# Tile 2 of queries and keys transposed by DMA, and five more products in TensorE's start-up

## The chip, the cores and the metric

The kernel runs on one core of one Trainium2 chip. The metric is the time of one execution on the device, in microseconds (us); lower is better. Every kernel is executed several times, and the median is compared.

## The reference

Two layers are chained. The first is attention with 8 batches, 8 heads, 576 positions and 64 values a head, in which a query sees only the keys at most 32 positions away. The second is a feed-forward layer over all 8 x 576 = 4608 tokens of 512 values, with a gated activation between its two products.

```python
scores = scale * np.matmul(q, k.transpose(0, 1, 3, 2))
mask = np.abs(pos[:, None] - pos[None, :]) <= 32
scores = np.where(mask, scores, -1000000000.0)
attn = softmax(scores)
x = np.matmul(attn, v)                   # (8, 8, 576, 64) -> (4608, 512)
h = x @ w_in                             # 512 -> 2048
out = (h * (1.0 / (1.0 + np.exp(-1.702 * h)))) @ w_out   # 2048 -> 512
```

## The kernel before

**Units, tiles, windows.** The 4608 tokens are laid end to end and shifted by 32. A *unit* is 128 tokens (36 units), a *window* two units, a *tile* of queries and keys 512 tokens or four units. For one unit the work is: `scores(u)` (TensorE, 32 small products of keys by queries into two PSUM banks, then exp on ScalarE), `band(u)` (VectorE multiplies by the 0/1 mask), `values(u)` (TensorE, weights times values), `norm(u)` (VectorE divides), `x_T(u)` (the result is transposed, by TensorE or by a DMA), `layer1` (TensorE, then the activation on ScalarE) and `layer2` or, from unit 8 on, `product`/`keep`/`result` (a scheme with seven products in place of eight). The first four units are masked in another way: `blind(u)` multiplies an identity by a tile `neg` of 0 and -30000 into the two score banks, and the scores are added on top of that.

**Queries and keys.** Scores need queries and keys with the head's values on the partitions, so both are transposed into two rings `qT` and `kT` of 1536 tokens (three tiles). Scores of unit u read the keys of unit u and 64 more, and queries from 32 to 160 after the unit's start. There are two ways to fill the rings.
- *By TensorE*: `load_heads` (four neighbouring tokens a partition, pieces of four tokens), `pair_heads` (a copy that puts two heads side by side), and `rows_T` (four transposes on TensorE into a PSUM bank, then one copy into the ring: VectorE for keys, ScalarE for queries). Tiles "A" and "B" (together tile 0), 1 and 2 go this way.
- *By transfer*: `load_rows` (one token a partition, chunks of 128 tokens) and `rows_X` (a DMA transpose of one chunk from SBUF into the ring, issued on SP). Tiles 3 to 8 go this way.

All loads are cast from f32 on their way and are issued on POOL's queue. SP issues the DMA transposes and the output stores; it is in order, so that a transpose whose load has not landed holds whatever stands behind it.

**The order of the work** is written out by hand: there is no scheduler, and each engine's instructions run in the order of the program text. `head()` holds the loads, units 0 to 6, layer 1 of windows 0 to 2 and layer 2 of units 0 to 3. `window(w)` follows from w = 4 on; window 4 begins with the scores of units 7, 8 and 9, all of which read tile 2. `feed(w)` issues transposes for later windows; in window 4 it also copies the first 64 keys and 32 queries of tile 3 to the ring's end (L714, L715), which the scores of unit 11 read. Near the start, `keep_busy` issues products of zeros, whose results nobody reads.

**PSUM.** Eight banks under four tags: "h" (2), "o" (1), "a" (4), "t" (1). Tile B's eight groups of transposes take turns on "h", "t" and "o", and wait for the copies out of them.

Of the kernel before, what the change touches and what calls it, by code (L numbers as in the profile page):

```python
# [21 lines left out]
SQ = 64  # L22
# [5 lines left out]
class _Kernel:  # L28
# [181 lines left out]
    def setup_neg(self):  # L210

        pool = self.nc.gpsimd
        self.neg = self.cst.tile([128, 2, SQ], BF16, name="neg")
        pool.memset(self.neg, 0.0)
        for b in range(2):
            for half in range(2):
                sign = 1 if half == b else -1
                ap = self.neg[64 * half:64 * half + 64, b, :]
                pool.affine_select(out=ap, in_=ap, compare_op=ALU.is_ge, fill=-30000.0, base=0,  # L219
                                   pattern=[[-sign, SQ]], channel_multiplier=sign)  # L220

    def blind(self, u):

        sc = self.sc[u] = [self.bank("a", [128, 8, SQ], F32, f"sc{eo}") for eo in range(2)]
        neg = self.neg.rearrange("k (o b) s -> k o b s", o=1).to_broadcast([128, 4, 2, SQ])
        for eo in range(2):
            self.nc.tensor.matmul(sc[eo].rearrange("k (h b) s -> k h b s", b=2), self.ident, neg,
                                  start=True, stop=False, skip_group_check=True)
# [192 lines left out]
    def head(self):  # L421

        nc, dve, act, pool = self.nc, self.nc.vector, self.nc.scalar, self.nc.gpsimd
        for hp in range(2):
            self.load_raw("k", hp, nc.sync)
            self.load_raw("q", hp, act)
        self.setup()
        for c in "kq":
            self.load_heads("A", c, (4, 8))
        self.setup_neg()  # L430
        for m in range(3):
            self.load_v(m)
        for c in "kq":
            self.load_heads("B", c)
        self.load_v(3)
        self.load_v(4, 0)
        for c in range(4):
            self.load_w_in(c)
        self.odd_v(2, pool)
        self.odd_v(3, pool)  # L440
        for c in (0, 2):
            self.load_w_out(c)
        self.setup_mask()
        self.cut_mask()
        for c in "kq":
            self.load_heads(1, c)
        self.load_w_out(1)
        self.load_v(4, 1)
        for m in range(5, 7):
            self.load_v(m)  # L450
        self.load_w_out(3)
        self.load_v(7)
        for c in "kq":
            self.load_heads(2, c)
        self.keep_busy(8)
        for hp in range(2):
            self.pair_heads("k", "A", hp, dve, self.stage["k", "raw", hp])
            self.pair_heads("q", "A", hp, act, self.stage["q", "raw", hp])
        for hp in range(4):
            self.rows_T("k", "A", hp, "ht"[hp % 2], dve)  # L460
            self.rows_T("q", "A", hp, "ho"[hp % 2], act)
            if hp < 2:
                self.blind(hp)
        self.scores(0)
        self.scores(1)
        self.odd_v(0, dve)
        self.odd_v(1, act)
        self.keep_busy(3, "h")
        self.values(0, "hh")
        self.norm(0)  # L470
        self.keep_busy(3, "o")
        self.x_T(0, "t", act)
        self.keep_busy(1, "o")
        self.values(1, "oa")
        self.norm(1)
        self.keep_busy(4, "a")
        self.x_T(1, "a", act)
        self.blind(2)
        self.blind(3)
        self.keep_busy(1, "h")  # L480
        for hp in range(4):
            self.pair_heads("k", "B", hp, dve)
        for hp in range(2):
            self.pair_heads("q", "B", hp, dve)
        for hp in range(4):
            self.rows_T("k", "B", hp, "htho"[hp], dve)
            if hp < 2:
                self.pair_heads("q", "B", hp + 2, dve)
            self.rows_T("q", "B", hp, "hoth"[hp], act)
        self.scores(2)  # L490
        self.scores(3)
        self.layer1(0, 0)
        self.values(2)
        self.norm(2)
        self.layer1(0, 1)
        self.values(3)
        self.norm(3)
        self.x_T(2, "t")
        self.layer1(0, 2, "a")
        self.x_T(3, "o")  # L500
        self.layer1(0, 3)
        for d in range(4):
            self.layer1(1, d)
        dve.tensor_copy(self.v_first, self.ve[0][0:64])
        dve.tensor_copy(self.k_first, self.kT[:, :, 0:64])
        dve.tensor_copy(self.q_first, self.qT[:, :, 0:32])
        for n in range(4):
            self.w_sums(n, 0)
        for c in "kq":
            for hp in range(4):  # L510
                self.pair_heads(c, 1, hp, dve)
        for t, d in ((0, 4), (0, 5), (1, 4), (1, 5), (0, 6), (0, 7), (1, 6), (1, 7)):
            self.layer1(t, d)
        l2 = [(lambda c=c, u=u: self.layer2(u, c, "hhot"[u], (dve, act)[u % 2])) for c in range(4) for u in range(4)]

        def run(n):
            for _ in range(n):
                l2.pop(0)()

        run(4)  # L520
        for hp in range(4):
            self.rows_T("k", 1, hp, "a", dve)
            self.rows_T("q", 1, hp, "a", act)
            run(1)
        self.scores(4)
        self.scores(5)
        for m in range(4, 7):
            self.odd_v(m, dve)
        self.band(4)
        run(3)  # L530
        self.band(5)
        run(1)
        self.values(4)
        self.norm(4)
        self.scores(6)
        run(1)
        self.gelu_table()
        self.values(5)
        self.norm(5)
        self.band(6)  # L540
        run(1)
        self.x_T(4, "a", act)
        run(1)
        self.x_T(5, "a", act)
        run(1)
        for c in "kq":
            for hp in range(4):
                self.pair_heads(c, 2, hp, pool)
        self.load_v(8)
        self.load_v(9)  # L550
        self.load_v(10)
        for c in "kq":
            self.load_rows(c, 3, (0, 1))
        self.layer1(2, 0)
        self.values(6)
        self.norm(6)
        for n in range(2):
            self.w_sums(n, 1)
        for d in range(1, 3):
            self.layer1(2, d)  # L560
        self.x_T(6, "a")
        self.layer1(2, 3)
        for hp in range(4):
            self.rows_T("k", 2, hp, "t", dve)
            if hp in (1, 2):
                self.w_sums(hp + 1, 1)
            self.rows_T("q", 2, hp, "o", act)
            self.layer1(2, 4 + hp)
        for m in (7, 8, 9):
            self.odd_v(m, dve)  # L570
        for m in (11, 12, 13):
            self.load_v(m)
        for c in "kq":
            self.load_rows(c, 3, (2, 3))
        for c in "kq":
            self.rows_X(c, 3, (0, 1))

    def window(self, w):
        nc, dve, sp = self.nc, self.nc.vector, self.nc.sync
# [193 lines left out]
```

## Time and profile before

| | us |
|---|---|
| median of 8 runs | 293.97 |
| lowest, highest | 293.18, 295.66 |
| profiled execution, its own time | 293.88 |
| its span, first to last instruction | 292.2 |
| TensorE busy | 285.6 (98%) |
| share of TensorE in the chain of waits | 92% |

The span is what the profile's times count from; the rest of the execution's own time lies around it. The page cuts the span in 40 slices of 7.3 us and gives each engine's busy share in tenths. The chain of waits is followed back from the last instruction: at every step to what released it. PE is TensorE's products, PEld its weight loads, DVE is VectorE, ACT ScalarE, SP the engine that only issues transfers. A transfer's time to landing counts from its issue to the semaphore that tells of its end. The chain, the timelines and the transfers are shown where the prediction uses them.

### The profile page before, as it was taken

How to read it: one execution, taken by the hardware profiler on the slowest of the kernel's cores; microseconds unless marked ns; L12 is line 12 of the kernel's file. 1: busy time of each engine (PE TensorE's matmuls, PEld its weight loads, DVE VectorE, ACT ScalarE, POOL GpSimd, SP SyncE). 2: the span in 40 equal slices, each digit the busy share in tenths (PEclk: the TensorE clock that was granted, in tenths of full speed). 3: DMA queues.
4: the chain of work that ended last, by engine and by line, in shares of the span. 5: the costliest groups of instructions: out<-in, count | busy, mean ns of one | idle time of the engine just before them, and what ended most of it. 6: DMA issues, size and time to landing. Idle time of an engine off the chain costs nothing.

```text
span 292.2 us, 9542 instructions
## 1 busy us (share of the span) xinstructions
PE 285.6 (98%) x4020; PEld 234.8 (80%) x4020; DVE 188.8 (65%) x552; ACT 185.2 (63%) x306; POOL 104.4 (36%) x146
## 2 busy tenths in 40 slices
PE   7989999999999999999999999999999999999995
PEld 2568765875888888888888888888888888888884
DVE  3653467787586858585858585858585858583353
ACT  4667547685776767676767675757575757575330
POOL 8875533998536351633333434242000000000000
PEclk9999999999999999999999999999999999999999
DMA  9999999999999999999999999999925230303012
GB/s 147 143 205 206 199 185 161 172 124 137 175 143 179 152 154 156 145 152 166 151 164 152 151 136 152 143 167 122 179 36 147 37 105 8 104 10 103 2 72 72
DMA packets 145291, 38.83 MB, mean 133 GB/s; under 512 B 129888, under 2 KB 140896, under 8 KB 145248
## 3 DMA queue, kind: packets, MB, share of 16 engines
q0 software_dynamic: 97696, 18.16, 87.5%
q1 hardware_dynamic: 47104, 19.67, 39.9%
q8 instruction: 31, 0.51, 0.7%
q10 hardware_dynamic: 448, 0.39, 0.5%
q14 instruction: 12, 0.10, 0.1%
HBM read 36.96 MB, written 9.44 MB: 159 GB/s over the span
## 4 chain that ended last, share of the span: by engine, by line
PE 92%; DMA 3%; POOL 2%; DVE 1%; issue 0%; ACT 0%; POOLq 0%; DVEq 0%
PE h_ps L313 43%; PE o_ps L375 32%; PE o_ps L325 7%; PE sc L245 4%; PE pv L273 4%; DMA qs<-in_q_dram 3%; PE tp L179 1%; POOL ve L160 1%; PE tp L300 1%; POOL ks L137 0%; DVE qc L105 0%; DVE o_sb L393 0%; POOL neg L219 0%; ACT qT L105 0%; DVE kT L105 0%
## 5 line engine op out<-in xcount | busy, mean ns | idle before, releaser
L313 PE MATMUL h_ps<-xT,w_in_sb 128*128 128x256 bf16 x1152 | 135.1, 273 | 0.0
L315 ACT ACTIVATE g<-h_ps 128x512 f16<-128x512 f32 x144 | 85.5, 595 | 73.7 <-PE h_ps L313 72.4
L313 PEld LDWEIGHTS <-w_in_sb 128*128 128x128 bf16 x1152 | 112.2, 98 | 13.4 <-DMA w_in_sb<-in_moe_w_in_dram 0.2
L160 POOL DMA_DIRECT2D ve<-in_v_dram x40 | 34.0, 857 | 76.6 <-PE pv L273 53.0
L375 PEld LDWEIGHTS <-gs 128*128 128x128 f16 x480 | 45.8, 98 | 6.0 <-issue 0.3
L375 PE MATMUL o_ps<-w_sum,gs 128*128 128x256 f16 x360 | 44.5, 273 | 0.0
L251 ACT ACTIVATE p<-sc 128x512 bf16<-128x512 f32 x72 | 37.2, 603 | 2.7 <-PE sc L245 2.5
L375 PEld LDWEIGHTS <-g 128*128 128x128 f16 x360 | 34.1, 98 | 4.5 <-ACT g L315 0.2
L352 DVE TENSOR_TENSOR gs<-g 128x512 f16<-128x512 f16 x30 | 12.7, 425 | 37.7 <-ACT g L315 37.6
L285 DVE TENSOR_TENSOR x<-pv,rec 128x256 bf16<-128x256 f32 x72 | 30.6, 424 | 2.5
L375 PE MATMUL o_ps<-w_out_sb,g 128*128 128x256 f16 x240 | 29.0, 273 | 0.0
L105 DVE COPY part<-o_ps 128x256 f32<-128x256 f32 x45 | 19.1, 424 | 13.0 <-PE o_ps L375 11.6
L393 DVE TENSOR_TENSOR o_sb<-o_ps,part 128x256 f32<-128x256 f32 x45 | 19.0, 422 | 12.0 <-PE o_ps L375 11.4
L262 DVE TENSOR_TENSOR p<-p,mask 128x512 bf16<-128x512 bf16 x64 | 25.0, 431 | 0.6 <-ACT p L251 0.6
L147 POOL DMA_DIRECT2D qs<-in_q_dram x27 | 23.0, 871 | 4.8 <-DMA ks<-in_k_dram 3.4
L147 POOL DMA_DIRECT2D ks<-in_k_dram x27 | 22.7, 854 | 4.4 <-DMA ve<-in_v_dram 4.0
L325 PE MATMUL o_ps<-w_out_sb,g 128*128 128x512 f16 x96 | 23.2, 380 | 0.0
L105 DVE COPY vo<-ve 64x528 bf16<-64x528 bf16 x65 | 20.7, 318 | 3.5 <-DMA ve<-in_v_dram 2.0
L251 ACT ACT_TABLE_LOAD x15 | 19.2, 1283 | 0.3
L412 ACT ACT_TABLE_LOAD x15 | 19.2, 1283 | 0.3
L284 DVE RECIPROCAL rec<-pv 128x4 f32<-128x4 f32 x72 | 12.6, 175 | 9.7 <-PE pv L273 9.7
L273 PEld LDWEIGHTS <-p 128*64 128x64 bf16 x576 | 11.3, 110 | 6.1 <-DVE p L262 3.6
(70 smaller groups left out, 246.3 us busy)
## 6 DMA issues: line engine op xcount, KB each, us to landing
out_dram<-o_sb SPq DMA_DIRECT2D x34, 256.0 KB, 3.0
ve<-in_v_dram POOLq DMA_DIRECT2D x32, 128.0 KB, 6.6
ks<-in_k_dram POOLq DMA_DIRECT2D x22, 128.0 KB, 7.4
qs<-in_q_dram POOLq DMA_DIRECT2D x22, 128.0 KB, 12.2
w_in_sb<-in_moe_w_in_dram POOLq DMA_DIRECT2D x4, 512.0 KB, 11.4
w_out_sb<-in_moe_w_out_dram POOLq DMA_DIRECT2D x4, 512.0 KB, 12.8
ve<-in_v_dram POOLq DMA_DIRECT2D x8, 64.0 KB, 6.9
ks<-in_k_dram POOLq DMA_DIRECT2D x7, 64.0 KB, 9.5
```

The lines of the kernel that those rows point to most:

```text
L105: (eng.copy if eng is self.nc.scalar else eng.tensor_copy)(out, in_)
L147: self.nc.gpsimd.dma_start(self.stage[key][off:off + m, n], src[b, :, s:s + m, :].rearrange("h s d -> s h d"))
L160: self.nc.gpsimd.dma_start(self.ve[m % NV][off:off + n, :, :self.D], self.v[b, :, s:s + n, :].rearrange("h s d -> s h d"))
L251: nc.scalar.activation(p[:, eo], sc[eo], AF.Exp, scale=self.scale)
L262: self.nc.vector.tensor_mul(pv, pv, msk.to_broadcast([128, 4, 2, SQ]))
L273: nc.tensor.matmul(acc[half][blk * 64:blk * 64 + 64, hh, :], p[:, h % 2, h // 2 * 2 + blk, :], vt[:, h, :D + 1], start=(hh == 0), stop=(hh ...
L285: nc.vector.tensor_mul(x[:, hs, :], acc[half][:, :, :D], rec[:, hs, :].to_broadcast([128, 4, D]))
L313: nc.tensor.matmul(hps[:, i, :], self.w_in_sb[:, kr, ff * 128:(ff + 1) * 128], self.xT[t][:, kr, :], start=(i == 0 and kr == 0), stop=(i = ...
L315: nc.scalar.activation(self.g[t][:, ffs[0]:ffs[1] + 1:ffs[1] - ffs[0], :], hps, AF.Gelu_apprx_sigmoid)
L325: nc.tensor.matmul(o_ps, self.g[t][:, ff, s * 128:(s + 1) * 128], self.w_out_sb[:, ff, :], start=(ff == 0), stop=(ff == self.NFF - 1))
L375: nc.tensor.matmul(self.part[t, key], x, y, start=(first and k == 0), stop=(k == 7), skip_group_check=True)
L412: self.nc.scalar.activation(self.spark, self.spark, AF.Gelu_apprx_sigmoid)
```

## The change

Three things are changed, all in `head()`.

1. Tile 2 is loaded with `load_rows` (8 transfers, chunks 0 and 1 of keys and queries, then 2 and 3) in place of `load_heads` (4 transfers), and `rows_X` transposes it by 8 DMA transposes on SP, which stand in the program behind the copies `v_first`, `k_first` and `q_first`. Its eight `pair_heads` copies on POOL and its eight `rows_T` on TensorE, VectorE and ScalarE are gone.
2. Loads move in POOL's queue: v of units 8 to 11 behind tile 2's loads; v of units 12 and 13 and then the whole of tile 3 to where the pairing copies of tile 2 stood. The DMA transposes of tile 3's first half move ahead of the last four `layer1` of window 2, and the last two `w_sums` on VectorE follow them.
3. A new `refill(u, n)` repeats `blind`'s mask product n times into the banks of unit u. As `start=True` overwrites the bank with the same values, the scores are the same. Four such products on unit 3 stand around the third key pair of tile B (one ahead, three behind), and a `keep_busy` ahead of tile B's transposes issues two products in place of one.

```diff
+    def refill(self, u, n):
+        neg = self.neg.rearrange("k (o b) s -> k o b s", o=1).to_broadcast([128, 4, 2, SQ])
+        for i in range(n):
+            self.nc.tensor.matmul(self.sc[u][i % 2].rearrange("k (h b) s -> k h b s", b=2), self.ident, neg,
+                                  start=True, stop=False, skip_group_check=True)
...
-        for c in "kq":
-            self.load_heads(2, c)
+        for chunks in ((0, 1), (2, 3)):
+            for c in "kq":
+                self.load_rows(c, 2, chunks)
...
-        self.keep_busy(1, "h")
+        self.keep_busy(2, "h")
...
         for hp in range(4):
+            if hp == 2:
+                self.refill(3, 1)
             self.rows_T("k", "B", hp, "htho"[hp], dve)
+            if hp == 2:
+                self.refill(3, 3)
...
+        for m in range(8, 12):
+            self.load_v(m)
+        for chunks in ((0, 1), (2, 3)):
+            for c in "kq":
+                self.rows_X(c, 2, chunks)
         for n in range(4):
             self.w_sums(n, 0)
...
-        for c in "kq":
-            for hp in range(4):
-                self.pair_heads(c, 2, hp, pool)
-        self.load_v(8)
-        self.load_v(9)
-        self.load_v(10)
-        for c in "kq":
-            self.load_rows(c, 3, (0, 1))
+        for m in (12, 13):
+            self.load_v(m)
+        for chunks in ((0, 1), (2, 3)):
+            for c in "kq":
+                self.load_rows(c, 3, chunks)
...
         self.layer1(2, 3)
-        for hp in range(4):
-            self.rows_T("k", 2, hp, "t", dve)
-            if hp in (1, 2):
-                self.w_sums(hp + 1, 1)
-            self.rows_T("q", 2, hp, "o", act)
-            self.layer1(2, 4 + hp)
+        for c in "kq":
+            self.rows_X(c, 3, (0, 1))
+        for n in range(2, 4):
+            self.w_sums(n, 1)
+        for d in range(4, 8):
+            self.layer1(2, d)
         for m in (7, 8, 9):
             self.odd_v(m, dve)
-        for m in (11, 12, 13):
-            self.load_v(m)
-        for c in "kq":
-            self.load_rows(c, 3, (2, 3))
-        for c in "kq":
-            self.rows_X(c, 3, (0, 1))
```

## The prediction

> **What bounds the kernel now.** First the page: busy shares, then the slices.
>
> ```profile
> PE 285.6 (98%) x4020; PEld 234.8 (80%) x4020; DVE 188.8 (65%) x552; ACT 185.2 (63%) x306; POOL 104.4 (36%) x146
> ...
> PE   7989999999999999999999999999999999999995
> ```
>
> A busy PE alone proves little, so I read the chain of waits next. Of its 292.2 us, 92% are TensorE (PE), and from 18 us to 287 us every piece is a PE piece. So what matters is the work in PE's queue, and each product taken out there is worth its chain time. Around the edit the chain reads (start, length, what):
>
> ```profile
> 56.85 0.45 PE tp L179 x8
> 57.30 0.87 PE h_ps L313 x8
> 58.17 0.45 PE tp L179 x8
> 58.62 0.87 PE h_ps L313 x8
> 59.49 0.45 PE tp L179 x8
> 59.94 0.87 PE h_ps L313 x8
> 60.81 0.45 PE tp L179 x8
> 61.26 0.87 PE h_ps L313 x8
> 62.13 0.73 PE sc L245 x64
> 62.86 2.69 PE o_ps L325 x12
> 65.56 0.38 PE sc L245 x32
> ```
>
> The four `tp` pieces are tile 2's transposes; `sc` at 62.13 are the scores of units 7 and 8, at 65.56 those of unit 9. They read tile 2. The timeline of PE shows the second place of the change, the only hole of note after 6 us (the last bracket is idle time and what ended it):
>
> ```profile
> 15.24 0.38 PE L418 MATMUL junk<-idle 128*128 128x512 bf16 x1
> 15.55 0.29 PE L179 MATMUL tp<-ident,kc 64*128 64x64 bf16 x4
> ...
> 16.07 0.28 PE L179 MATMUL tp<-ident,qc 64*128 64x64 bf16 x4
> 16.36 0.27 PE L179 MATMUL tp<-ident,kc 64*128 64x64 bf16 x4
> 17.23 0.27 PE L179 MATMUL tp<-ident,qc 64*128 64x64 bf16 x4 [0.59 <-DVE kT L105]
> ```
>
> Last the transfers, because tile 2 will depend on them. SP issues the DMA transposes one by one; tile 3's first four:
>
> ```profile
> 61.62 2.73 SPq L154 DMA_TRANSPOSE kT<-ks  x2
> 64.44 3.49 SPq L154 DMA_TRANSPOSE qT<-qs  x2
> ...
> DMA to landing us min/median/max: 6.5/7.9/9.3
> ...
> DMA to landing us min/median/max: 2.4/2.4/4.0
> ```
>
> The first landing line is that of all transposes into kT up to 110 us, the second of xT's from 215 to 270 us, when no load runs any more. A transpose takes 2.4 us when alone and 6.5 to 9.3 beside the loads.
>
> **What the Trainium skill says.** "DMA: Bandwidth & Descriptors", section "Issuing engines are not separate DMA queues": transfers issued by SP and by POOL end on the same 16 DMA engines and interleave. The trace agrees (2.4 against 7.9 us above). The same page, "Specifications", asks for at least 512 B per piece for full rate; tile 2's pieces shrink from 512 B to 128 B in SBUF. The trace agrees: from 57.5 to 62.5 us it moved 5642 such packets, 0.71 MB, 0.14 MB/us, against 0.49 MB in 2.5 us, 0.20 MB/us, in the 512 B pieces from 45 us. "TensorE: Matmul & The Clock Gate", Part 1: the clock halves after about one idle window (some 3.4 us, free-running), and Part 4 says that transposes do not count as busy in the same way. The trace shows the half rate only at the start (eight products of 512 columns in 3.27 us); at 12.84 us four take 1.04 us. It shows no fall of the clock near 16 us. The refills can protect against one in other executions, but this trace does not show it.
>
> **Part 1: tile 2's transposes leave TensorE.** 4 head pairs x (k and q) x 4 = 32 products of 219 ns, pipelined to 4 x 0.45 = **1.80 us** of the chain. Nothing else replaces them in PE's queue: a gain of 1.80 us, if tile 2 is in time. Gone too are 4 copies of 0.69 us on VectorE, 4 of 0.58 us on ScalarE, and on POOL 2.28 + 2.67 us of pairing copies. All of these lay beside PE and are worth nothing directly. The gelus behind layer 1's products (0.60 us each against 0.87 us of PE) keep up; the exp of unit 7 shifts with PE.
>
> **Part 2: five more products of 512 columns.** Mask products at 14.19 us were spaced 0.26 us apart. One refill fits ahead of the third k pair (free since 16.19) and makes it 0.1 us late, which is covered, since its copy waits for VectorE until 17.45. Three refills last 0.78 us, from about 16.57 to 17.35; the q pair behind them could start at 17.23. The extra junk product moves the first transposes from 15.55 to some 15.67, with VectorE busy to 15.97 anyway. Cost: 0 (all in holes) to 0.3 us (every overhang passed on to scores 2); I take **0.1**. A gain is not excluded: the runs spread from 293.18 to 295.66, and if a clock dip were behind the upper ones, the median could fall by up to 0.8 us, to its fastest run. I take 0 and keep 0.8 for the low end.
>
> **Part 3: the transfers.** On POOL, tile 2's loads become 8 issues of some 0.88 us (7.0 us) in place of 4 (0.59 + 0.88 + 0.58 + 0.77 = 2.8 us). POOL sat idle for 7.00 us before the first pairing copy, so the issues hide. It never seems to have more than eight transfers under way (the issue at 29.32 follows the landing, at 29.0, of the one eight back). v 8 to 11 move ahead, v 12, 13 wait for values 4 and 5 (49.5 us), with tile 3's loads queued behind them. Before, v 8 was issued only at 53.49.
>
> When is tile 2 there? The load ahead of it, v 7, lands at 35.13 + 10.6 = 45.8. A load of 128 tokens is 1024 pieces; at 5642 in 5 us that is 0.91 us alone; beside transposes I saw six such loads land from 66.3 to 75.4, 1.5 us each. So: k0 46.7, k1 47.6, q0 49, q1 50.5, k2 52, k3 53.5, q2 55, q3 56.5. SP issues each transpose (1.3 to 1.4 us) in that order: the 4th (q1) at about 51.1, the 7th (q2) at 55.6. To landing the four quoted took 6.5, 7.2, 8.5 and 7.2 us, mean 7.4; later ones up to 9.8. That gives:
> - scores 8 need chunks 0 and 1, at 62.4 - 1.8 = 60.6; the 4th lands at 58.5 (57.6 to 60.9). In time by 2.1 us, at worst 0.3 late.
> - scores 9 need chunk 2, at 65.5 - 1.8 = 63.7; the 7th lands at 63.0 (62.1 to 65.4). In time by **0.7 us**, at worst 1.7 late.
>
> So I cost this at 0, with 0 to 1.7 us kept. Behind the eight transposes on SP stand the four output stores (issued from 49.89 before, now from about 58); their buffers are wanted again only after 65 us. Then come tile 3's transposes, first half: its loads now queue behind 12 small-piece loads plus v 12 and 13, and I get their landing at 66.5 to 69.3 and the last transpose issued at 70.7 to 72. Two things hang on this. VectorE's copy of the ring's end (77.44, now 75.6) waits for the third of them, at about 76.8; behind it are the g sums, which had 1.52 us of idle time ahead of them, so 1.2 us is absorbed. And unit 9's x_T, which stands behind them on SP, goes from 72.57 to about 73.4, and with its 7.9 us lands at 81.3; layer 1 wants it at 83.25 - 1.8 = 81.45. Just in time; kept: 0 to 1 us.
>
> **Sum.** -1.80 + 0.1 + 0 = -1.7 us on the profiled execution (293.88 us, its span 292.2 and 1.7 around it): 292.2. The median of the runs is 293.97, 0.09 more: **292.3 us**.
>
> **The rivals.**
> - *Tile 2 is somewhat late* (0.3 to 3.2 us of waiting). The margin of 0.7 us is smaller than the spread of a transpose's landing (6.5 to 9.8), and eight in a row were never seen. The trace has groups of four. With 0.7 us of waiting the time is 293.0; the whole case runs from 292.5 to 295.4. This is no change that could be told: 0.5% is about 1.5 us, what a measurement of this kernel can tell from none.
> - *Slower: scores 9 wait for the seventh transpose.* Landings in the quoted group were up to 2.65 us apart. At that distance from the first (46.9 + 6.5 = 53.4), the seventh lands at 69.3, and PE stands 5.6 us at `sc` L245: 292.3 + 5.6 = 297.9. It decides from a landing at 65.4 on (gain gone) and at 66.9 (over 0.5% slower). For it: 12 loads of small pieces run against the transposes without a break. Against: other groups landed 1.0 to 2.1 us apart.
> - *The gain is paid later*: x_T of unit 9 late by up to 1 us at window 5's first layer 1, 293.3. Against: the transfers then have had 25 us to even out.
> - *It does not do what it says*: if the clock already dips in most executions, the refills alone bring up to 0.8 us more, 291.5. The profile speaks against it.
>
> **Chances.** In time, or late by under 0.3 us: 0.42 (faster by over 0.5%, below 292.5). Late by some: 0.33 (within 0.5%). Slower by over 0.5%: 0.25. The range starts at 291.4 (1.80 gained on the fastest run) and goes to 296.5, which leaves the far part of the slow case out. The likeliest case alone is 291.4 to 292.6.
>
> **What would show it.** In the chain of the changed kernel no `tp` L179 after 43 us, and `sc` near 60.3 and 63.8 with no DMA piece ahead of them. A piece "DMA kT<-ks" or "DMA qT<-qs" just ahead of a score, or idle time of PE or PEld at L245, shows the rivals at once, with their price. PE's gap at 17.23 should be nearly filled and scores 2 still start near 17.9. Eight more transposes on SP between 47 and 58 us. The prediction is wrong if the seventh lands after 64 us, or if a layer 1 of window 5 waits for xT.

## The result, and the profile after

| | before | after |
|---|---|---|
| median, us | 294.06 (32 runs) | 297.66 (11 runs) |
| lowest, highest of the 11 runs | | 295.37, 299.71 |
| profiled execution, its own time | 293.88 | 295.37 |
| its span | 292.2 | 293.7 |

The ratio is 1.0122, 95% interval 1.0097 to 1.0147: **slower by 3.6 us**, where 1.7 us of gain were forecast. The profiled execution is the quickest of those runs, only 1.49 us above the one before, so it shows part of the loss. Line numbers of the kernel after are higher by 7 (L245 is now L252, L313 is L320, L325 is L332), those of the ring's end by 8 (L714 and L715 are L722 and L723); L105, L154 and L179 keep theirs.

The page first, busy shares and the slices of TensorE:

```profile
PE 285.3 (97%) x3993; PEld 233.5 (80%) x3993; DVE 186.8 (64%) x548; ACT 183.4 (62%) x302; POOL 103.5 (35%) x142
...
PE   7999999999979999999999999999999999999995
```

Before, a 7 and an 8 stood at the start and nothing but nines until the end. Now the 8 of the third slice is a 9 (the hole near 17 us is filled) and slice 12, 80.8 to 88.1 us, has become a 7. The share of one slice in forty says where to look. The chain of waits after, from 54.9 to 85 us, in columns of start, length and what:

```profile
54.94 9.48 DMA qT<-qs
64.42 0.04 issue
64.46 0.41 PE sc L252 x28
...
69.98 0.86 PE o_ps L332 x4
70.84 3.51 PE h_ps L320 x32
...
76.23 0.08 DVE gs L365
76.31 7.86 DMA xT<-x
84.16 0.14 issue
84.30 1.03 PE h_ps L320 x8
```

Two DMA pieces stand where every piece was PE before. The seventh transpose of tile 2 (54.94, then 9.48 us) releases 28 of the 32 scores of unit 9. The transpose of x of unit 9 (76.31, then 7.86 us) releases the first layer 1 of window 5 at 84.30. The list of TensorE's waits prices both (total, times, longest, in us):

```profile
PE h_ps L320 <- DMA xT<-x: 2.0, 1, 2.0
...
PE sc L252 <- DMA qT<-qs: 0.4, 1, 0.4
PE pv L280 <- issue: 0.3, 1, 0.3
```

Set against the timeline before, the account of this execution is:

| first start of | before | after | difference |
|---|---|---|---|
| scores of unit 2 | 17.80 | 18.07 | +0.27 |
| scores of unit 7 | 62.06 | 60.47 | -1.59 |
| layer 1 at window 4's end | 71.64 | 70.68 | -0.96 |
| layer 1 of window 5 | 83.08 | 84.30 | +1.22 |
| end | | | +1.5 |

So the forecast gain was there at 60 us, 1.59 us of it, and was spent at three places, and more with it: 0.6 us around unit 9's scores, 2.2 us at window 5, and 0.3 us at a small stall at 144.6 us. How the second wait comes about stands in SP's own timeline after (start, time in the queue, line, what, count):

```profile
45.94 2.60 SPq L154 DMA_TRANSPOSE kT<-ks  x2
48.58 3.37 SPq L154 DMA_TRANSPOSE qT<-qs  x2
52.07 2.78 SPq L154 DMA_TRANSPOSE kT<-ks  x2
54.94 3.46 SPq L154 DMA_TRANSPOSE qT<-qs  x2
58.49 2.88 SPq L337 DMA_DIRECT2D out_dram<-o_sb  x4
68.03 3.20 SPq L154 DMA_TRANSPOSE kT<-ks  x2
71.32 2.73 SPq L154 DMA_TRANSPOSE qT<-qs  x2
74.14 0.70 SPq L337 DMA_DIRECT2D out_dram<-o_sb  x1
74.95 2.69 SPq L303 DMA_TRANSPOSE xT<-x  x2
```

Tile 2's eight transposes are out at 58.4. Then SP stands until 68.03, because tile 3's first load, issued on POOL at 53.25, lands only at 67.97. Four transposes, a store and the x_T of unit 8 follow; unit 9's x_T is the second in the last line, issued at 76.31, and lands at 84.16.

VectorE shows two more waits that go with the new transfers (the bracket is idle time and what ended it):

```profile
66.29 0.69 DVE L105 COPY o_sb<-o_ps 128x512 f32<-128x512 f32 x1 [2.26 <-PE pv L280]
...
78.06 0.55 DVE L723 COPY qT<-qT 128x128 bf16<-128x128 bf16 x1 [1.17 <-DMA qT<-qs]
```

The first starts 0.09 us after the first output store lands (66.20), although the trace names a product as its releaser; the second is the copy to the ring's end. No wait of TensorE in the list above names either of them.

Between executions more differs than one profile can show. The mean granted clock of TensorE, the share of its full clock that it was given, is recorded for each. Of 12 executions after (the 11 and one more), 6 had it full and took 296.50 us in the median, and 6 had it some 0.6% lower (one 1.1%) and took 299.19. The kernel before was run again with each group of experiments; of these 180 executions 121 had it full (294.01) and 59 lower (295.38). A fall of 0.6% over 293 us is 3.5 us at half clock, worth 1.75 us of lost work. This gives three parts to explain: 2.5 us between the kernels at full clock, 2.7 us more in half of the executions after, and a fall of the clock that a third of those before also had. The profiled execution after is itself 1.1 us quicker than the median at full clock, so that the usual waits may be longer than those that it shows.

### The profile page after: what moved, and what is told of

It is laid out like the page before. It is cut to its first block, busy times and chain, and to the rows that moved or that the text cites. A ratio compares the mean times of both kernels' runs of the same rounds, so it can differ in the third digit from the quotient of the medians.

```text
span 293.7 us, 9490 instructions
## 1 busy us (share of the span) xinstructions
PE 285.3 (97%) x3993; PEld 233.5 (80%) x3993; DVE 186.8 (64%) x548; ACT 183.4 (62%) x302; POOL 103.5 (35%) x142
## 4 chain that ended last, share of the span: by engine, by line
PE 73%; DMA 16%; POOL 4%; SPq 3%; issue 1%; DVE 1%; ACT 0%; POOLq 0%; DVEq 0%
PE h_ps L320 35%; PE o_ps L382 30%; DMA w_out_sb<-in_moe_w_out_dram 4%; DMA ks<-in_k_dram 3%; PE pv L280 3%; DMA qT<-qs 3%; SPq L154 3%; PE sc L252 3%; DMA xT<-x 3%; DMA ve<-in_v_dram 3%; PE o_ps L332 2%; POOL ve L160 1%; POOL vo L105 1%; POOL w_out_sb L113 0%; POOL qs L137 0%
## 5 line engine op out<-in xcount | busy, mean ns | idle before, releaser
L320 PE MATMUL h_ps<-xT,w_in_sb 128*128 128x256 bf16 x1152 | 134.5, 273 | 2.0 <-DMA xT<-x 2.0
L320 PEld LDWEIGHTS <-w_in_sb 128*128 128x128 bf16 x1152 | 112.2, 98 | 15.7 <-issue 2.3
L147 POOL DMA_DIRECT2D qs<-in_q_dram x31 | 26.3, 861 | 16.1 <-DMA ks<-in_k_dram 5.4
L147 POOL DMA_DIRECT2D ks<-in_k_dram x31 | 26.4, 859 | 6.9 <-DMA ve<-in_v_dram 4.4
L105 DVE COPY part<-o_ps 128x256 f32<-128x256 f32 x45 | 19.1, 424 | 13.3 <-PE o_ps L382 11.9
L400 DVE TENSOR_TENSOR o_sb<-o_ps,part 128x256 f32<-128x256 f32 x45 | 19.0, 422 | 12.1 <-PE o_ps L382 11.4
L269 DVE TENSOR_TENSOR p<-p,mask 128x512 bf16<-128x512 bf16 x64 | 24.2, 417 | 2.9 <-ACT p L258 2.7
L332 PE MATMUL o_ps<-w_out_sb,g 128*128 128x512 f16 x96 | 23.2, 380 | 0.0
L105 DVE COPY vo<-ve 64x528 bf16<-64x528 bf16 x65 | 21.7, 335 | 1.7
```

Of the source, the lines that this page charges most:

```text
L105: (eng.copy if eng is self.nc.scalar else eng.tensor_copy)(out, in_)
L147: self.nc.gpsimd.dma_start(self.stage[key][off:off + m, n], src[b, :, s:s + m, :].rearrange("h s d -> s h d"))
L269: self.nc.vector.tensor_mul(pv, pv, msk.to_broadcast([128, 4, 2, SQ]))
L320: nc.tensor.matmul(hps[:, i, :], self.w_in_sb[:, kr, ff * 128:(ff + 1) * 128], self.xT[t][:, kr, :], start=(i == 0 and kr == 0), stop=(i = ...
L332: nc.tensor.matmul(o_ps, self.g[t][:, ff, s * 128:(s + 1) * 128], self.w_out_sb[:, ff, :], start=(ff == 0), stop=(ff == self.NFF - 1))
```

## The experiments

**The theories.** The first is *late transposes*: TensorE waits for tile 2 and, above all, for x_T of unit 9 behind tile 3, and the wait itself makes the clock fall. Its rivals are *dear products* (the five products of the change cost more than their holes are worth) and *small pieces* (the new loads in 128 B pieces and their order crowd out others, whether or not the transposes follow). Later a fourth was needed, *the next wait*: behind each wait that is removed stands another, because they hang on one queue. In the recorded expectations, theory Q is *late transposes*, R *dear products*, and C0 and C are about the clock. The time that each experiment is compared with is that of the kernel before in the same group of runs.

### e1: the five products alone

The kernel before, with `refill`, the second junk product and the four refills, nothing else.

```diff
-        self.keep_busy(1, "h")
+        self.keep_busy(2, "h")
+            if hp == 2:
+                self.refill(3, 1)
...
+            if hp == 2:
+                self.refill(3, 3)
```

> The kernel before with the five extra products alone (refills and the second junk product), tile 2 as before. Theory Q (the loss is a late queue of transfers): their cost is what the first score showed, about 0.2 us, so 294.2 +- 0.3 us, clock 1.000. Theory R (the refills upset the start): 296 us or more. Theory C0 (the runs of before already dip in the clock and the refills cure it): under 293.7 us.

Measured: 295.07 us (22 runs) against 294.36, ratio 1.0023 (1.0010 to 1.0037). No execution had a lowered clock, where 13 of 43 in the same group did without the products. At full clock that is 1.02 us above the kernel before (294.05). Scores of unit 2 start at 18.35 (17.80 before), and a stall of 0.73 us follows at 159.54. So *dear products* holds in part: they cost some 0.5 us in place and give a steady clock in return. The next experiment shows that the 3.6 us are not theirs.

### e2: the change without the five products

```diff
-        self.keep_busy(2, "h")
+        self.keep_busy(1, "h")
...
-                self.refill(3, 1)
...
-                self.refill(3, 3)
```

> The change without its five extra products (tile 2 by transfer and the moved loads only). Theory Q: 297.4 us, 0.2 less than the changed kernel, and the clock still 0.994 in about half of the runs. Theory R: back to 293 us, below the kernel before by the 1.8 us of transposes.

Measured: 297.83 us (6 runs), ratio 1.0115 (1.0078 to 1.0152), as slow as the whole change; 2 of the 6 had a lowered clock. TensorE's waits in its profile:

```profile
PE h_ps L320 <- DMA xT<-x: 1.8, 1, 1.8
PE sc L252 <- DMA qT<-qs: 1.4, 1, 1.4
...
PE sc L252 <- DVE qT L719: 1.2, 1, 1.2
PE pv L280 <- issue: 1.0, 2, 0.9
```

The same two waits for transfers, together larger here (3.2 us against 2.4), and the ring's end has now reached TensorE (third line). With the stalls of 1.0 us (fourth line) they come to 5.4 us, against a gain of 1.8: 3.6 us, where the profiled execution lies some 4.1 us above that of the kernel before and the 4 executions at full clock 3.3 us in the median.

### e3: unit 8's and unit 9's x transposed by TensorE

The change, with x_T of these two units among window 4's layer 1 on TensorE instead of on SP's queue.

```diff
-            self.x_T(a)
...
-            self.x_T(b)
...
-            run(l1, 8)
+            run(l1, 3)
+            self.x_T(a, "t", dve)
+            run(l1, 2)
+            self.x_T(b, "t", dve)
+            run(l1, 3)
```

> The changed kernel, but x of units 8 and 9 is transposed by TensorE between products of layer 1 in window 4 (two groups of 0.22 us) in place of two DMA transposes on SP. Theory Q: the wait of about 2 us for xT at the first layer 1 of window 5 is gone, and the clock's dip with it if the dip follows from that wait: 293.0 to 293.8 us, clock 1.000 in all runs. If the dip comes from elsewhere (scores of unit 9 or the start): 294.5 to 295.5 us with 0.994 in half of the runs. Theory R: 297 us, unchanged.

Measured: 294.14 us (14 runs), ratio 0.9992 (0.9973 to 1.0012), no lowered clock in 14. The wait at window 5 is gone, and one wait for a transfer remains:

```profile
PE sc L252 <- DMA qT<-qs: 0.8, 1, 0.8
```

It costs eight more small products, two pieces of 0.22 us in the chain, and still takes 3.5 us off the change, to a little above the 293.0 to 293.8 us that I expected. The x_T of these two units, of which unit 9's lands last, carry most of the loss, and the falls of the clock with it.

### e7: the hole of window 5 filled with products of zeros

The wait stays, but TensorE works in it.

```diff
+            if w == 5:
+                self.keep_busy(9, "h")
             run(l1)
```

> The changed kernel with nine products of zeros (9 x 0.216 = 1.9 us) put in TensorE's queue ahead of window 5's first layer 1, into the hole of 2.0 us; the wait for xT itself is not touched. Theory C (the hole makes TensorE's clock fall to half in about half of the runs, at some 1.7 to 2.7 us): clock 1.000 in nearly all runs, 296.3 to 296.8 us, the level of those runs of the changed kernel whose clock stayed full. Against it (the dip has another cause): 297.7 us or more, with clocks of 0.994 as before.

Measured: 296.42 us (13 runs), ratio 1.0064 (1.0040 to 1.0088), no lowered clock in 13. TensorE's timeline:

```profile
80.96 1.92 PE L382 MATMUL o_ps<-w_sum,gs 128*128 128x256 f16 x16
82.72 2.11 PE L425 MATMUL junk<-idle 128*128 128x512 bf16 x9
84.69 1.03 PE L320 MATMUL h_ps<-xT,w_in_sb 128*128 128x256 bf16 x8
```

Layer 1 is as late as ever (84.69), nothing useful was added, and the time is near that of the change's executions at full clock (296.50), now with a full clock in every execution. **Idleness in this hole makes the clock fall.** What is left, 2.4 us over the kernel before at full clock (294.02), is the waits and the products less the gain.

### e6: tile 2 loaded in the new way, but transposed by TensorE

The loads of 128 B pieces, their order, the moved loads and the five products stay. The eight DMA transposes go, and 32 products on TensorE stand again between the layer 1 of window 2: `rows_P` does four of them into one PSUM bank, and one copy from there into the ring.

```diff
-        for chunks in ((0, 1), (2, 3)):
-            for c in "kq":
-                self.rows_X(c, 2, chunks)
...
-        for d in range(4, 8):
-            self.layer1(2, d)
+        for hp in range(4):
+            self.rows_P("k", 2, hp, "t", dve)
+            self.rows_P("q", 2, hp, "o", act)
+            self.layer1(2, 4 + hp)
```

> The changed kernel with tile 2 still loaded as rows in pieces of 128 B, and all loads in their moved places, but transposed by TensorE (32 transposes, 1.8 us of PE) in place of the eight DMA transposes. It tells the small pieces from the transposes. If the eight transposes are what delays tile 3's loads and xT (theory Q, transposes): no wait in window 5, 294.9 to 295.5 us (the kernel before and some 1 us for the refills as e1 has it), no dip of the clock. If the small pieces are: xT of unit 9 late again, 297.5 to 299.5 us.

Measured: 294.09 us (22 runs, 293.66 to 294.88), ratio 0.9986 (0.9969 to 1.0002), no lowered clock. SP's timeline:

```profile
60.46 2.67 SPq L154 DMA_TRANSPOSE kT<-ks  x2
63.23 2.65 SPq L154 DMA_TRANSPOSE qT<-qs  x2
68.21 0.34 SPq L345 DMA_DIRECT2D out_dram<-o_sb  x1
71.78 2.60 SPq L311 DMA_TRANSPOSE xT<-x  x2
```

Without the eight transposes tile 3's first is issued at 60.46 instead of 68.03 and unit 8's x_T at 71.78 instead of 74.95. No wait is left in window 5. *Small pieces* falls: the pieces and the new order hurt nobody until the eight transposes run beside them. The Trainium skill, "DMA: Bandwidth & Descriptors", section "Issuing engines are not separate DMA queues", says that transfers issued by different engines end on the same 16 DMA engines; here tile 3's first load landed at 67.97 with the eight transposes and at 60.39 without them, and only 1.0 us of the difference is a later issue.

The time is below the 294.9 to 295.5 us that I expected: with the same five products as e1, e6 stands at the level of the kernel before at full clock (294.02). So the price of the products is less than e1's 1.02 us.

### e4 and e5: better orders of the loads

e4 puts the loads of tile 3's first half ahead of v 11 to 13. e5 does that, and loads and transposes tile 2 in the order chunks 0 and 1, then k2, q2, then k3, q3, so that the keys and queries of unit 9 come ahead of those of unit 10.

```diff
-        for m in range(8, 12):
-            self.load_v(m)
+        for m in range(8, 11):
+            self.load_v(m)
+        for c in "kq":
+            self.load_rows(c, 3, (0, 1))
+        self.load_v(11)
...
-        for chunks in ((0, 1), (2, 3)):
-            for c in "kq":
-                self.load_rows(c, 3, chunks)
+        for c in "kq":
+            self.load_rows(c, 3, (2, 3))
```

and in e5, for tile 2, both around `load_rows` and around `rows_X`:

```diff
-        for chunks in ((0, 1), (2, 3)):
+        for chunks in ((0, 1), (2,), (3,)):
```

> The changed kernel, but in POOL's queue the loads of tile 3's first half stand ahead of those of v 11, 12 and 13. Theory Q: they land some 4 us earlier, the transposes of tile 3 leave SP by about 70 us in place of 74, xT of unit 9 lands by 81 in place of 84.2, and the wait of window 5 is mostly gone: 293.3 to 294.3 us. If SP is not held by these loads but by the engines' total load: 296 to 298 us, unchanged.

> The kernel of e4_tile3_loads_first, with tile 2's third chunk of keys and queries loaded and transposed ahead of the fourth (k0 k1 q0 q1 k2 q2 k3 q3), so that the chunk that unit 9's scores need is the 6th transpose and not the 7th. Theory Q: it lands some 1.4 us earlier and the wait of 0.4 to 1.4 us ahead of those scores is gone: 0.3 to 0.8 us below e4's, 293.3 to 293.7 us. If that wait is not in the timed runs: 294.0, as e4.

Measured: e4 294.04 us (14 runs), ratio 0.9989 (0.9967 to 1.0011); e5 294.00 us (22 runs), ratio 0.9984 (0.9967 to 1.0001). One of e4's 14 executions and none of e5's 22 had a lowered clock. Both get the loss back and neither gets the gain. In e4's profiled execution (295.47 us, well above its median) x_T of unit 9 still lands at 84.07 and costs a wait of 1.6 us. In e5 scores of unit 9 start at 63.99 without a wait, but now the store's landing, seen above, does reach TensorE. VectorE's timeline of e5, which names it this time:

```profile
66.67 0.69 DVE L105 COPY o_sb<-o_ps 128x512 f32<-128x512 f32 x1 [2.48 <-DMA out_dram<-o_sb]
```

The masks of units 8 and 9 stand behind this copy, and their values behind the masks: 0.6 to 0.9 us lost. This is *the next wait*.

### e8 and e9: the stores between the transposes

e8 is e5 with the last two transposes of tile 2, those of chunk 3, behind the four output stores. e9 is e8 with three of the five products: no refill ahead of the third key pair, one junk product.

```diff
-        for chunks in ((0, 1), (2,), (3,)):
+        for chunks in ((0, 1), (2,)):
             for c in "kq":
                 self.rows_X(c, 2, chunks)
...
+        for c in "kq":
+            self.rows_X(c, 2, (3,))
         for m in (12, 13):
             self.load_v(m)
```

> The kernel of e5_chunk_order with the last two transposes of tile 2 (chunk 3, which only unit 10's scores read) behind the four output stores on SP. In e5's profile the stores landed at 66.6 us and held the buffer of the next output, and with it VectorE's masks and TensorE's values of units 8 and 9, for some 0.6 to 0.9 us. Theory Q, third wait: that is gone, 293.1 to 293.6 us. If the stores were not on the path: 294.0, as e5.

> e8_stores_between with three extra products in place of five: only the three refills behind the third key pair. If the clock needs only the hole filled (theory C): clock 1.000 throughout and 0.2 to 0.5 us less than e8, as the first scores start that much earlier. If five are needed: clocks of 0.994 in about a third of the runs, as in the kernel before.

Measured: e8 294.20 us (22 runs), ratio 1.0002 (0.9983 to 1.0020); e9 294.37 us (22 runs), ratio 1.0014 (0.9989 to 1.0039). No gain, against what I expected. In e8 everything up to 80 us was early (scores of unit 9 at 63.82, layer 1 of window 4 at 69.97), yet x_T of unit 9 arrived when it always had. TensorE's timeline of e8, whose profiled execution had a lowered clock:

```profile
79.66 1.92 PE L382 MATMUL o_ps<-w_sum,gs 128*128 128x256 f16 x16
83.99 1.03 PE L320 MATMUL h_ps<-xT,w_in_sb 128*128 128x256 bf16 x8 [2.41 <-DMA xT<-x]
...
87.45 1.65 PE L320 MATMUL h_ps<-xT,w_in_sb 128*128 128x256 bf16 x8
```

and the table of two stretches (start:end, length, busy time of PE, PEld, DVE, ACT and POOL with counts; third from the end is the granted clock):

```profile
80.00:85.00 5.00, 2.59 (x25) 1.93 (x24) 1.86 (x6) 2.62 (x5) 1.76 (x2) 1.00 1.73 176
85.00:88.50 3.50, 3.50 (x46) 2.64 (x46) 1.89 (x7) 0.60 (x1) 0.88 (x1) 0.54 1.62 155
```

This is the fall itself: after 2.41 us of waiting TensorE runs at half clock from 85.3 to 88.7 us, and the same eight products take 1.65 instead of 1.03 us. Executions with it took 296.62 us in e8 (3 of 22) and 297.04 in e9 (7 of 22), some 2.7 to 3 us above the others. The fall itself is not worth that much: from the first layer 1 of window 5 to the end this execution takes 210.92 us and the profiled one of the kernel before 209.09, and 0.39 of the 1.83 us between them is a stall at 146.05. That leaves some 1.4 us for the fall. The rest would be a longer wait in the executions that fall; no profile shows it. The Trainium skill, "TensorE: Matmul & The Clock Gate", Part 1, states that the clock halves after an idle window of some 3.4 us which runs freely, and is full again after a busy one as long; the 3.4 us of this fall agree, but here a hole of 2.41 us was enough.

For *the next wait* this is the plainest case: the earlier TensorE is (layer 1 at window 4's end at 70.68 in the change, 69.97 in e8, 69.56 in e9), the longer this one wait (2.0, 2.4 and 2.6 us). The transfer's end is set by SP's queue and not by TensorE. SP's timeline of e8:

```profile
71.37 2.52 SPq L154 DMA_TRANSPOSE qT<-qs  x2
73.98 0.57 SPq L337 DMA_DIRECT2D out_dram<-o_sb  x1
74.65 3.08 SPq L303 DMA_TRANSPOSE xT<-x  x2
```

The load of queries ahead of the first line was issued at 51.56 and landed at 71.35; in the change it was issued at 58.44 and landed at 71.03. An earlier place in POOL's queue did not bring it earlier. Unit 9's x_T, again the second in the last line, landed at 83.85.

### e10: three products alone

```diff
+            if hp == 2:
+                self.refill(3, 3)
```

> The kernel before with the three refills alone. e1 (all five) stood 1.0 us above those runs of the kernel before whose clock stayed full. If that is the products' own time on the path: a part of it, 294.3 to 294.7 us. If it is late fetches of instructions, which fall elsewhere when the count of instructions changes: it can be anything from 293.9 on, with no relation to the products' time.

Measured: 294.25 us (14 runs), ratio 1.0006 (0.9991 to 1.0021), no lowered clock in 14; scores of unit 2 start at 17.57. Three products keep the clock as steady as five. Against the kernel before at full clock (293.79 in this group) they lose 0.46 us, where five lost 1.02.

### e11 and e12: no wait left, with and without the products

e11 joins e9 and e3: the order of loads, the stores between, three products, and x_T of units 8 and 9 on TensorE (the edit of e3). e12 is e11 without the three products:

```diff
-            if hp == 2:
-                self.refill(3, 3)
```

> e9_three_refills (tile 3's loads first, chunk order, stores between, three refills) with x of units 8 and 9 transposed by TensorE as in e3. Every wait seen so far on TensorE is then without its cause: xT (2.4 to 2.6 us in e8 and e9), scores 9, the stores. Theory Q: 1.8 us of transposes gone, 0.45 us for x on TensorE, no dip of the clock: 292.4 to 293.0 us against 294.1 for the kernel before. If something else of the transfers waits next (unit 11's copy of the ring's end, values): 293.5 us or more.

> e11_no_wait_left without any refill. If the dips of the kernel before (clock 0.994 in about a third of its runs, 1.4 us each) come from the hole near 17 us: clock of 0.994 in about a third of the runs, the runs with full clock at e11's level or up to 0.2 us below it, the median some 0.3 us above e11. If they do not come from there: no dips, as in e11.

Measured: **e11 292.66 us** (18 runs) against 294.35, ratio 0.9937 (0.9921 to 0.9953), no lowered clock in 18. It beats both kernels. TensorE's timeline and waits of e11:

```profile
79.98 1.92 PE L382 MATMUL o_ps<-w_sum,gs 128*128 128x256 f16 x16
81.74 1.04 PE L320 MATMUL h_ps<-xT,w_in_sb 128*128 128x256 bf16 x8
```

```profile
PE junk L425 <- DVE ve L86: 1.3, 1, 1.3
PE tp L179 <- DVE kc L105: 0.7, 2, 0.4
PE tp L307 <- DVE x L292: 0.3, 1, 0.3
PE tp L179 <- ACT qc L105: 0.2, 1, 0.2
PE tp L179 <- DVE kT L105: 0.2, 1, 0.2
```

Layer 1 of window 5 follows at once, at 81.74 (83.08 before, 84.30 after the change). No wait for a transfer is in the list; what is left lies in the start-up. e12: 292.68 us (19 runs), ratio 0.9949 (0.9934 to 0.9965), at full clock 292.58 (16 executions), at the lowered one 294.14 (3). That settles the sum within 0.2 us: -1.80 for tile 2 and +0.44 for the x transposes is -1.36, and at full clock e12 lies 1.54 us under the kernel before (294.12). The hole of 0.58 us near 17 us is back, and lowered clocks are too: 3 of 19, against 0 of 18 in e11. These two counts alone are too small to tell apart.

## Why the prediction was wrong

**Part 1, -1.80 us: right.** Scores of unit 7 came 1.59 us earlier, with +0.27 for the products at the start; e12 confirms the size where nothing waits for a transfer.

**Part 2, +0.1 us: too small, and its other side missed.** Scores of unit 2 came 0.27 us later in the change and 0.55 in e1, and in all profiles with five products they start from 17.90 to 18.57. With three (17.57 to 17.69) they start about where they do with none (17.38 to 17.80). So the two products at the front, the refill ahead of the third pair and the second junk product, account for most of it: the later pairs stand behind one another on one engine, and an overhang is passed on. The sentence that the trace "shows no fall of the clock near 16 us" was true of that one execution, but a third of all executions had a lower mean clock, and with the hole filled none had (0 of 22 in e1, 0 of 14 in e10). The rival in which the products cure this was right in kind; alone, with five products, it ends at +0.7 us, not -0.8.

**Part 3, transfers at 0: the steps that failed.**
- *Tile 2 in time*: the loads landed 1.0 us apart in the mean where up to 1.5 was reckoned, 0.7 to 3.8 us ahead of the estimates (q2 at 51.17 instead of 55), and the seventh transpose was issued at 54.94 (forecast 55.6), since SP takes 1.3 us for each. Its 9.48 us to landing were sized at 7.4. It landed at 64.42, 0.7 us past the need of 63.7, and cost a wait of 0.4 us. That it came so close was luck: early loads and slow transposes nearly cancelled. The rival "somewhat late" named this at the right place.
- *The stores "are wanted again only after 65 us"*: they landed from 66.20 on, 7.7 us after issue. In the change they can have cost at most the 0.2 us around unit 9's scores that the listed wait does not explain; in e5 they were the bound. I had given them no landing time.
- *The failing step*: unit 9's x_T "goes from 72.57 to about 73.4, and with its 7.9 us lands at 81.3", with 0 to 1 us kept for it. The 7.9 us were right (7.86). The issue was 2.9 us later, at 76.31. Tile 3's first load landed at 67.97 (forecast from 66.5), the last of its four transposes was issued at 72.65 (forecast 70.7 to 72) and held SP until 74.06, which is 0.7 us past 73.4; then a store and unit 8's x_T, which I had left out, took the other 2.2 us. Both stood ahead of unit 9's x_T before the change too. It landed at 84.16, and TensorE waited 2.0 us. The rival "the gain is paid later" had this place right and sized it at up to 1 us.
- *No price for the clock*: a wait was costed at its own length. With one of 2.0 us in its profile, half of the executions after had a lowered clock and took 2.7 us more, of which the clock itself is some 1.4 to 1.75 us. These executions took the median from 296.5 to 297.66.

The argument against "the gain is paid later", that the transfers "have had 25 us to even out", fails as well. A late load holds an in-order queue, and what stands behind it cannot even out.

**What would have shown it beforehand**: writing down SP's queue as a list, instruction by instruction with issue times, from 45 to 77 us, as was done for the loads. The prediction did it for eight transposes and stopped.

**Open.** At full clock e1 is 1.02 us slower than before, of which 0.55 are seen at scores 2; the stall of 0.73 us at 159.54 would cover the rest, and e10's profile has one of 0.64 us at 158.95, but each was seen in one execution. The 1.1 us by which the median at full clock after lies above the profiled execution are in no profile. Where in an execution the lower clock of the kernel before sits was not seen either; that it goes with the hole near 17 us is inferred from e1 and e10 against the kernel before. What share transposes and loads each have in the late landings was not taken apart.

## What to carry to other kernels

When work moves from a full engine to transfers, write out the whole in-order queue that issues them, up to the next thing the full engine needs, and not only to the thing that was moved. A gain upstream of a transfer whose end another queue sets turns into a longer wait for it; take that transfer out of the queue (e11) or the gain is not kept. A wait of 2 to 2.4 us on TensorE can cost another 1.4 to 1.75 us through a clock that falls to half, in some executions only: read the clock of all runs, not of the one profile.

## What the runs showed of the hardware

- The clock fell after a hole of 2.41 us (half rate for 3.4 us, e8), and the runs suggest that even the hole of 0.58 us among transposes of 64 columns near 17 us is enough at times (59 of 180, and 3 of 19 in e12). With products of zeros or repeated products in the hole it was not seen (0 of 13 in e7, 0 of 22 in e1, 0 of 14 in e10).
- While loads in 128 B pieces ran, a DMA transpose took 6.5 to 9.8 us to land (the kernel before), 9.48 in the change and up to 11.4 in e8, and an output store 7.5 to 8.3 us (the change, 55 to 80 us).
- TensorE's stalls with the label "issue", of 0.3 to 0.9 us, came at the same places of its instruction stream, counts equal to 191 to 194 modulo 256, and a 16 KB packet on the queue for instructions had started some 2 us ahead of the stall each time (in the change: packet at 142.3, stall from 144.3 to 144.62). It may be that the next instructions came late; no experiment tested it.
